# Two attention blocks in one kernel: later branch hints, early transfers awaited before the branch, and an instruction order from new costs

## The chip, the core and the metric

The kernel runs on one core of a Trainium2 chip. A core has five engines that work side by side, each on its own stream of instructions: TensorE (PE, matrix products, whose weight loads the profile lists as PEld), VectorE (DVE), ScalarE (ACT), GpSimd (POOL) and SyncE (SP, which here only issues transfers). They meet through semaphores. On-chip data lies in SBUF; products land in PSUM, which has eight banks of 128 x 512 32-bit numbers.

The metric is the device time of one execution in microseconds, lower is better. It is given as the median of several runs. Beside it stands one execution that the hardware profiler recorded; its span goes from the first to the last recorded instruction.

## The reference

Two attention blocks are computed from separate inputs, and their outputs stand side by side. Both have 2048 rows, width 1024 and 32 heads of 32.

```python
def _A_ref(x, wqkv, wo):
    qkv = transpose((x @ wqkv).reshape(B, S, 3, H, Dh), 2, 0, 3, 1, 4)
    q, k, v = qkv[0], qkv[1], qkv[2]
    p = softmax(einsum('bhqd,bhkd->bhqk', q, k) * Dh ** -0.5)
    o = einsum('bhqk,bhkd->bhqd', p, v)
    return merge_heads(o) @ wo

def _B_ref(x, wq, wk, wv, wo, beta):      # N = 4 segments of L = 512 rows
    phi = lambda t: where(t > 0, t + 1.0, exp(t))
    g = sigmoid(beta);  M = 0;  z = 0
    for s in range(N):
        p = softmax(einsum('bhqd,bhkd->bhqk', qs, ks) * scale + causal_mask)
        a_dot = einsum('bhqk,bhkd->bhqd', p, vs)
        a_mem = (phi(qs) @ M) / (phi(qs) @ z + 1e-06)
        outs.append(g * a_mem + (1.0 - g) * a_dot)
        M = M + phi(ks).T @ vs;  z = z + phi(ks).sum(rows)
    return merge_heads(outs) @ wo

return concatenate([a, b], axis=-1)
```

A is full attention over 2048 keys. B is causal attention within segments of 512 rows, plus a memory that each segment reads and then updates.

## The kernel before, in words

**Tiling.** Heads go in groups of four (g = 0 to 7), so that a group fills 128 partitions. For A a unit is a group and 256 query rows: 64 units, each with 8 pieces of 256 keys. For B a unit (a "block") is a segment and a group: 32 blocks, each in 3 pieces. A piece of scores is computed transposed, keys on the partitions, into pairs of PSUM banks: three pairs serve the scores (`PAIRS`, banks 0 to 5), and two single banks (6 and 7, the pool `side`) serve everything else, that is projections, P·V, the memory products and the output rows. ScalarE reads a pair of banks, 128 x 1024, and writes the exponentials as bf16 into a slot of `PT` (line 1097). No maximum is subtracted; instead, the reciprocals of the row sums are checked at the end against a range (`ranges`, lines 1378 on), and the result is a flag in SBUF. Where the flag is not zero every engine branches to a second, slow program that subtracts maxima (`shifted`). With the inputs here it is not entered.

**Masks and powers.** Of a B block's three pieces two are masked by VectorE (line 1107) and one by GpSimd (line 1109), after the exponential. For phi the exponential is made on VectorE, without ScalarE: `power` (lines 1127 to 1135) takes the number apart into exponent and fraction with two integer operations and evaluates a polynomial with three `scalar_tensor_tensor` steps. `b_mem` (line 857) calls it for phi(k) and phi(q), 48 times in all. `exps_dve`, the other caller, is used only for pieces listed in `off`, and that list is empty because the parameter `off` is 0; `oks` is read only to fill it.

**The order.** The kernel has no dynamic scheduling on the chip. While it is built, a planner (`Sched`) simulates the five engines with a cost for each operation, and writes each engine's stream in the order in which its simulated queue takes operations. An operation goes when its inputs are ready by the plan; among several ready ones the lowest `prio` goes first. Costs are the `cost=` of each `do(...)`, in microseconds; `dve(n)` is n x 0.00088 + 0.14 for VectorE. Semaphore waits are put in afterwards where an operation needs another engine's result, so a wrong cost does not make a wrong result, but an instruction that stands too early in its engine's stream holds up everything behind it.

Score products have priority 0. Other products by TensorE have a due position: `pos` counts finished score pieces, and a job that is due at `due` has priority 10 + (due - pos) until it has begun, and at most 4 from then on. P·V has priority 5 while fewer than 7 slots of `PT` are free, and else the parameter `pv`. The parameters that set due positions or release:

- `span`: over how many positions ahead of a group's first A scores the nine projections of its K, Q and V are spread
- `mem`, `memM`: the due position of a block's memory products (`mem` behind the block's first scores) and of its memory update (`memM` behind that)
- `od`, `ob`: the due position of the first of a segment's eight B output rows, and the step from one to the next (`out_B`)
- `wob`: the position at which the 2 MB transfer of `WoB`, the output weights of B, is issued

The list of score pieces itself (`batches`) depends on `rate`, `lead` and `b0`.

**The end of each stream.** `emit` writes for each engine: the whole stream (`play`), a wait for the flag, a load of the flag into a register (line 435), and a branch on it (line 437). In `play` a branch hint, an instruction that tells the engine's sequencer about the branch to come, is put ahead of the operation that stands `HINT[name]` places before the stream's end; where the stream is shorter than that, ahead of the first. Behind the branch SP waits until the last transfer on each of 24 channels has landed (`drain`, line 147). A transfer takes the next channel in turn and a semaphore of its own, so 24 semaphores are awaited.

## Time and profile before

| | |
|---|---|
| median of 10 runs | 1106.36 us (1105.52 to 1109.06) |
| the profiled execution's own time | 1107.8 us |
| its span | 1106.1 us |
| mean granted TensorE clock | 0.994 |
| ScalarE before its first exponential | 10.92 us |
| last exponential's end | 1098.64 us |
| operations that GpSimd, SP play | 227, 285 |
| branch hints, at us | GpSimd 0.75, SP 0.79, PE 0.87, VectorE 600.5, ScalarE 823.0 |

An execution is longer than its span because something lies around the recorded instructions. A line of instruction groups has the source line, the engine, the operation, output and inputs with their shapes, the count, the busy time and the mean duration of one, and then the engine's idle time just ahead of these instructions with what ended it. Durations of neighbours overlap, since an engine starts an operation before the one ahead has written its last results; the time from start to start is the better price of one. "ps" stands for PSUM, whatever the bank.

### The profile page before, as it was taken

How to read it: one execution, taken by the hardware profiler on the slowest of the kernel's cores; microseconds unless marked ns; L12 is line 12 of the kernel's file. 1: busy time of each engine (PE TensorE's matmuls, PEld its weight loads, DVE VectorE, ACT ScalarE, POOL GpSimd, SP SyncE). 2: the span in 40 equal slices, each digit the busy share in tenths (PEclk: the TensorE clock that was granted, in tenths of full speed). 3: DMA queues.
4: the chain of work that ended last, by engine and by line, in shares of the span. 5: the costliest groups of instructions: out<-in, count | busy, mean ns of one | idle time of the engine just before them, and what ended most of it. 6: DMA issues, size and time to landing. Idle time of an engine off the chain costs nothing.

```text
span 1106.1 us, 54139 instructions
## 1 busy us (share of the span) xinstructions
PE 1039.2 (94%) x25177; PEld 535.3 (48%) x25177; DVE 749.1 (68%) x1569; ACT 1078.7 (98%) x1188; POOL 123.0 (11%) x231
## 2 busy tenths in 40 slices
PE   8999999999999998989999998999999999899998
PEld 4545455444444444444444544445444444454544
DVE  2366657555778779877788789787856767643333
ACT  6999999999999999999999999999999999999997
POOL 2010001001002011111112111111111111100000
PEclk9999899999999999999999999999999999999999
DMA  9632533242212322243212232412142221201111
GB/s 187 103 70 46 122 69 66 46 95 58 65 31 51 58 58 49 47 81 63 60 46 50 47 74 55 87 28 56 41 70 55 37 55 27 84 32 36 36 38 64
DMA packets 213767, 67.49 MB, mean 61 GB/s; under 512 B 202786, under 2 KB 210978, under 8 KB 213538
## 3 DMA queue, kind: packets, MB, share of 16 engines
q1 hardware_dynamic: 212066, 63.07, 27.2%
q8 instruction: 198, 3.24, 1.2%
q10 hardware_dynamic: 1472, 0.92, 0.3%
q14 instruction: 31, 0.25, 0.1%
HBM read 36.70 MB, written 8.39 MB: 41 GB/s over the span
## 4 chain that ended last, share of the span: by engine, by line
ACT 66%; PE 23%; DVE 7%; DMA 2%; issue 1%; POOL 0%; SPq 0%; DVEq 0%
ACT PT L1097 65%; PE ps L717 8%; PE ps L1212 6%; PE ps L1066 5%; PE ps L1301 3%; DMA VB<-VT 1%; PE ps L1348 1%; DVE we L1133 1%; DVE we L1134 1%; DVE VT L722 1%; DMA WA<-in_A_wqkv_dram 1%; ACT OTA L1097 1%; DVE ze L1132 0%; DVE PH L1135 0%; DMA VA<-VT 0%
## 5 line engine op out<-in xcount | busy, mean ns | idle before, releaser
L1097 ACT ACTIVATE PT<-ps 128x1024 bf16<-128x1024 f32 x1164 | 1057.7, 1153 | 10.7 <-PE ps L1066 10.1
L1212 PE MATMUL ps<-PT,ones 128*32 128x256 bf16 (+2 forms) x4784 | 283.6, 268 | 0.0
L1212 PE MATMUL ps<-PT,VA 128*32 128x256 bf16 x4016 | 241.8, 274 | 3.1 <-DVE OD L1254 0.7
L1066 PE MATMUL ps<-QA,KA 32*128 32x256 bf16 x4096 | 210.4, 274 | 34.0 <-ACT PT L1097 28.7
L717 PE MATMUL ps<-xA,WA 128*32 128x512 bf16 (+1 forms) x3232 | 204.3, 371 | 5.6 <-DMA WA<-in_A_wqkv_dram 1.1
L717 PE MATMUL ps<-xB,WB 128*32 128x512 bf16 x3072 | 205.5, 383 | 4.4 <-DVE amem L913 1.0
L1066 PEld LDWEIGHTS ps<-QA,KA 32*128 32x128 bf16 x4096 | 62.7, 92 | 207.8 <-ACT PT L1097 191.6
L1212 PEld LDWEIGHTS ps<-PT,ones 128*32 128x32 bf16 x4784 | 127.8, 97 | 29.7 <-issue 13.3
L1212 PEld LDWEIGHTS ps<-PT,VA 128*32 128x32 bf16 x4016 | 106.9, 96 | 43.7 <-issue 24.0
L717 PEld LDWEIGHTS ps<-xA,WA 128*32 128x32 bf16 x3232 | 74.4, 96 | 78.3 <-issue 25.6
L717 PEld LDWEIGHTS ps<-xB,WB 128*32 128x32 bf16 x3072 | 70.9, 96 | 77.9 <-issue 33.6
L1254 DVE COPY OD<-ps 128x512 f32<-128x512 f32 x127 | 86.5, 682 | 25.7 <-PE ps L1212 25.2
L722 DVE CAST VT<-ps 128x512 bf16<-128x512 f32 x64 | 44.0, 688 | 69.5 <-PE ps L717 52.8
L1306 DVE CAST outsb<-ps 128x512 bf16<-128x512 f32 x56 | 38.6, 690 | 72.0 <-PE ps L1301 69.8
L1109 POOL TENSOR_TENSOR PT<-PT,mask 128x256 bf16<-128x256 bf16 x64 | 45.6, 713 | 354.0 <-ACT PT L1097 352.6
L722 DVE CAST KQB<-ps 128x512 bf16<-128x512 f32 x64 | 44.1, 688 | 44.3 <-PE ps L717 42.2
L1301 PE MATMUL ps<-WoB,OTB 128*32 128x512 bf16 x1024 | 66.3, 381 | 0.7 <-DVE OD L1254 0.6
L853 POOL COPY VZ<-VB 64x256 bf16<-64x256 bf16 x64 | 28.5, 446 | 344.8 <-DMA VB<-VT 322.5
L1260 DVE STREAM_TRANSPOSE OD<-Rall 128x256 f32<-128x256 f32 x127 | 55.7, 439 | 3.0
L1257 DVE STREAM_TRANSPOSE Dt<-OD 128x256 f32<-128x256 f32 x127 | 55.3, 436 | 2.0
L1212 PE MATMUL ps<-PT,VB 128*32 128x192 bf16 (+2 forms) x768 | 45.1, 243 | 9.4 <-DVE OD L1254 3.0
L1301 PE MATMUL ps<-xA,OTA 128*32 128x512 bf16 x832 | 53.2, 381 | 0.2 <-DVE outsb L1306 0.2
(111 smaller groups left out, 880.8 us busy)
## 6 DMA issues: line engine op xcount, KB each, us to landing
WB<-in_B_wk_dram SPq DMA_DIRECT2D x32, 256.0 KB, 3.0
WB<-in_B_wq_dram SPq DMA_DIRECT2D x32, 256.0 KB, 3.0
WB<-in_B_wv_dram SPq DMA_DIRECT2D x32, 256.0 KB, 3.6
out_dram<-outsb SPq DMA_DIRECT2D x63, 128.0 KB, 1.8
WA<-in_A_wqkv_dram SPq DMA_DIRECT2D x23, 256.0 KB, 3.0
WoB<-in_B_wo_dram SPq DMA_DIRECT2D x1, 2048.0 KB, 9.9
xA<-in_A_wo_dram SPq DMA_DIRECT2D x1, 2048.0 KB, 9.5
OTA<-in_A_x_dram ACTq DMA_DIRECT2D x2, 256.0 KB, 4.5
```

What stands on the lines that cost most here:

```text
L717: ins = e.matmul(self.ps[32 * c:32 * c + 32, bank, lo:hi], W[:, i, 32 * c:32 * c + 32], x(i)[:, lo:hi], start=st, stop=sp)
L722: return e.tensor_copy(dst, self.ps[:, bank, 0:n])
L853: yield do("POOL", lambda e, j=j: e.tensor_copy(self.VZ[H * j:H * j + H, j:4:2, :], V[0:H, j:4:2, 0:P]), r=[("VB", n % 2)], w=["VZ"], cost ...
L1066: ins = e.matmul(out, l, r, start=a, stop=z)
L1097: yield do("ACT", lambda e: e.activation(to, self.ps[:, pr[0]:pr[1] + 1, 0:n], ACTF.Exp, scale=sc), r=[("ps", bk) for bk in pr], w=keys, c ...
L1109: yield do("POOL", lambda e: e.tensor_tensor(d, d, m, ALU.mult), r=keys + ["mask"], w=keys, cost=0.25 + sz * 0.0014, prio=0)
L1212: ins = e.matmul(out, l, r, start=st, stop=sp)
L1254: yield do("DVE", lambda e: e.tensor_copy(OD[:, :], self.ps[:, OB, :]), r=[("ps", OB)], w=[("OD", x), ("Rb", x)], cost=dve(2 * QU), prio=0 ...
L1257: yield do("DVE", lambda e: e.transpose(Dt[:, :], Rb), r=[("Rb", x)], w=[("Dt", x)], cost=dve(QU), prio=self.par["fp"], hold=0.15)
L1260: yield do("DVE", lambda e: e.transpose(Rb.rearrange("p (a b) -> p a b", b=32), self.spread(Rc)), r=[("Rc", ui % 64)], w=[("Rb", x)], cost ...
L1301: ins = e.matmul(self.ps[32 * c:32 * c + 32, bank, lo:hi], lhs(j)[:, 32 * c:32 * c + 32], W(j)[:, lo:hi], start=st, stop=sp)
L1306: return f(self.outsb[ob][:, :], self.ps[:, bank, :])
```

## The change

Four things are changed.

1. `HINT`: TensorE's hint goes from the first operation to the 600th from the end, GpSimd's number from 999 to 230 and SP's from 999 to 250. VectorE's and ScalarE's numbers stay.
2. `drain` can leave out the last few transfers, or take only these. SP now awaits all channels but those of the three last-planned transfers ahead of the flag, and these three behind the branch.
3. Parameters: `mem` -2 to 0, `memM` 6 to 2, `span` 50 to 60, `pv` 18 to 14, `ob` 1 to 4, `od` 8 to 4, `wob` 60 to 80, `oks` (1, 4, 6) to (1, 3, 5).
4. Planned costs: a mask on VectorE, `dve(sz)` to 0.12 + sz x 0.00055 (for 256 columns 0.365 to 0.261, for 512 columns 0.591 to 0.402); a mask on GpSimd, 0.25 to 0.4 plus sz x 0.0014 (0.608 to 0.758); each of the three polynomial steps of a power, 0.57 to 0.61.

The order of all five streams is planned anew from 3 and 4.

```diff
-    def drain(self, eng):
-        last = [op for op in self.ch_last if op is not None]
-        for op in sorted(last, key=self.all.index):
+    def drain(self, eng, but=0):
+        last = sorted([op for op in self.ch_last if op is not None], key=self.all.index)
+        for op in last[but:] if but < 0 else last[:len(last) - but]:
             eng.wait_ge(self.ch_sem[op.dma], 16 * self.ch_n[op.dma])
...
-HINT = {"PE": 99999, "ACT": 300, "DVE": 700, "POOL": 999, "SP": 999}
+HINT = {"PE": 600, "ACT": 300, "DVE": 700, "POOL": 230, "SP": 250}
...
-    par = dict(b=(16, 12, 9), mem=-2, memM=6, span=50, rate=0.6, ahead=28, sl=7, pv=18, ob=1, lead=6, b0=1, bpos=16, wob=60, mg=0.05, off=0, oks=(1, 4, 6), sh=4, pd=4, o0=4, od=8,
+    par = dict(b=(16, 12, 9), mem=0, memM=2, span=60, rate=0.6, ahead=28, sl=7, pv=14, ob=4, lead=6, b0=1, bpos=16, wob=80, mg=0.05, off=0, oks=(1, 3, 5), sh=4, pd=4, o0=4, od=4,
...
                 loc = self.R.play(eng, name, HINT[name])
+                if name == "SP":
+                    self.R.drain(eng, 3)
                 self.R.after(eng, self.flagop)
                 v = eng.value_load(self.flag[0:1, 0:1])
...
                 if name == "SP":
-                    self.R.drain(eng)
+                    self.R.drain(eng, -3)
...
             if self.par["mk"][k]:
-                yield do("DVE", ... ALU.mult), ... cost=dve(sz), prio=self.par["mp"])
+                yield do("DVE", ... ALU.mult), ... cost=0.12 + sz * 0.00055, prio=self.par["mp"])
             else:
-                yield do("POOL", ... ALU.mult), ... cost=0.25 + sz * 0.0014, prio=0)
+                yield do("POOL", ... ALU.mult), ... cost=0.4 + sz * 0.0014, prio=0)
...
-        yield do("DVE", lambda e: e.scalar_tensor_tensor(w, uf, C2, uf, ALU.add, ALU.mult), ... cost=0.57, prio=pd)
-        yield do("DVE", lambda e: e.scalar_tensor_tensor(w, w, C1, uf, ALU.add, ALU.mult), ... cost=0.57, prio=pd)
-        yield do("DVE", lambda e: e.scalar_tensor_tensor(ap, w, C0, pf, ALU.add, ALU.mult), ... cost=0.57, prio=pd)
+        yield do("DVE", lambda e: e.scalar_tensor_tensor(w, uf, C2, uf, ALU.add, ALU.mult), ... cost=0.61, prio=pd)
+        yield do("DVE", lambda e: e.scalar_tensor_tensor(w, w, C1, uf, ALU.add, ALU.mult), ... cost=0.61, prio=pd)
+        yield do("DVE", lambda e: e.scalar_tensor_tensor(ap, w, C0, pf, ALU.add, ALU.mult), ... cost=0.61, prio=pd)
```

## The prediction

> **What bounds the kernel now.** I read the busy table first, then the two groups that carry most of ScalarE's and the masks' work, then the waits of ScalarE, then the run cut into stretches, and last the records of the final 8 us.

> ```profile
> PE 1039.2 (94%) x25177; PEld 535.3 (48%) x25177; DVE 749.1 (68%) x1569; ACT 1078.7 (98%) x1188; POOL 123.0 (11%) x231
> ...
> L1097 ACT ACTIVATE PT<-ps 128x1024 bf16<-128x1024 f32 x1164 | 1057.7, 1153 | 10.7 <-PE ps L1066 10.1
> ```

> ScalarE (ACT) is busy 98% of the span with the exponentials of line 1097, so nothing that the other engines do can save more than ScalarE's idle time. Its exponentials start 0.904 us after one another (median in the trace; 1153 ns is the latency of one, and they overlap). Their number and their order come from the list of score pieces, which the change leaves alone, so the busy 1078.7 us stay. What can move is where ScalarE waits:

> ```profile
> ACT PT L1097 <- PE ps L1066: 10.1, 19, 1.5
> ACT WoB L1097 <- PE ps L1066: 7.9, 2, 7.3
> ACT outsb L1306 <- PE ps L1301: 3.3, 1, 3.3
> ```

> Scores come late 19 times, 10.1 us in all, the worst time 1.5 us. The other two rows are the start (the first exponential begins at 10.92) and the tail. Cut into stretches, ScalarE's busy time beside the length shows where the idle lies:

> ```profile
> 155.00:355.00 200.00, 198.93 (x221) 1.00 0.27 59
> ...
> 515.00:660.00 145.00, 142.23 (x158) 1.00 0.24 54
> 660.00:830.00 170.00, 169.90 (x189) 1.00 0.29 58
> 830.00:876.00 46.00, 43.04 (x48) 0.96 0.27 48
> ```

> Columns are the stretch, its length, busy time (instructions), TensorE's clock, DMA share and GB/s. Idle is 1.07, 2.77, 0.10 and 2.96 us here. The span of 1106.06 is 10.92 of start, 1076.33 of exponentials, 11.39 of idle between them (9.92 of it from 125 to 1042, which is 1.08% of these 917 us) and 7.42 of tail after the last exponential at 1098.64. The profiled execution took 1107.8, 1.7 more than its span and 1.4 more than the median of the runs, 1106.36; I work out differences on the profiled execution and take them from the median.

> **What the idle is made of.** For each gap of ScalarE I looked for the last wait of TensorE (PE) before it. (a) Six times, at 387, 444, 566, 599, 652 and 875, the chain of waits goes through the steps of a power on VectorE (DVE, lines 1130 to 1135) and then a bank that VectorE hands back late; with the small gap that follows at 654 these are 3.47 us. (b) At 846 and 849, 2.66 us, TensorE waited 1.9 us for GpSimd's (POOL's) VZ, whose transfer had taken 5.17 us instead of its median 2.5. (c) At 214, 267, 329, 508, 571, 1022, 1030 and 1043, 2.5 us, TensorE never waited; other work simply stood before the scores. The rest lies at 125 to 155 and at 37.7.

> **The costs that the order is built with.**

> ```profile
> L1133 DVE SCALAR_TENSOR_TENSOR we<-ue 128x512 f32<-128x512 f32 x48 | 34.7, 722 | 0.0
> ...
> L1107 DVE TENSOR_TENSOR PT<-PT,mask 128x256 bf16<-128x256 bf16 x64 | 20.3, 316 | 7.8 <-ACT PT L1097 7.1
> L1107 DVE TENSOR_TENSOR PT<-PT,mask 128x512 bf16<-128x512 bf16 x32 | 15.0, 468 | 11.0 <-ACT PT L1097 10.8
> ```

> A power's three steps were planned at 0.57 us and now at 0.61; from start to start the trace has 0.72. So 0.04 of the missing 0.15, about a quarter, is made good. Masks on VectorE were planned at 0.365 and 0.591 and now at 0.261 and 0.402; start to start they take 0.209 and 0.342, so the surplus shrinks from 0.16 and 0.25 to 0.05 and 0.06. Masks on GpSimd go from 0.608 to 0.758; the page has a mean of 0.713 (64 of them, 45.6 us). These edits add no instruction; they move what the planner puts next to them. For group (a) the gain lies between 0 (a quarter of the error is not enough to move the bank's handback) and 3.47 (all six go). I take half, 1.7, since the cost moves the right way in each, but by less than the error.

> VectorE runs a step of a power longer when GpSimd works beside it, which no cost of either version knows:

> ```profile
> 438.67 0.43 DVE L1132 TENSOR_SCALAR ze<-ze 128x512 int32<-128x512 int32 x1
> 439.01 1.16 DVE L1133 SCALAR_TENSOR_TENSOR we<-ue 128x512 f32<-128x512 f32 x1
> 440.09 0.41 DVE L1107 TENSOR_TENSOR PT<-PT,mask 128x512 bf16<-128x512 bf16 x1
> 440.43 1.16 DVE L1134 SCALAR_TENSOR_TENSOR we<-we,ue 128x512 f32<-128x512 f32 x1
> ```

> GpSimd's masks ran from 438.83 for 0.79 and from 440.23 for 0.81. Over the run, line 1133 takes 684 ns alone (median of 39) and 873 beside a GpSimd operation (median of 9, worst 1178). [...]

> **The places.** pv 14 instead of 18 puts P·V ahead of projections that are due more than 4 positions away (before: more than 8). span 60 asks for A's projections up to 10 positions sooner. mem and memM move the memory matmuls two later and the update two sooner. od and ob spread B's output rows over 4 to 32 positions instead of 8 to 15. wob moves the 2 MB load of WoB by 20 positions, some 36 us at two exponentials each; at 117.2 it took 9.9 us to land, and it has to be there for line 1301 first at 282, so the move itself costs nothing, but the transfers behind it on SP's queue (PKt 5.9 instead of 2.5) are late at another place. oks is read only with off above zero, and off is 0: nothing. No instruction or byte is added. What all this does to the idle no row shows; the stretches bound it. At the rate of 660 to 830 (0.06%) the 917 us would have 0.5 idle, 9.4 less; at that of 515 to 660 (1.91%) 17.5, 7.6 more. Ordinary long stretches (155 to 355 has 0.54%) would give 5.0. Between these I credit half of (b), 1.3, since a transfer of twice its median is an accident of one order that another need not repeat, and 0.5 of (c), since spread output rows stand less densely before the scores at 1022 to 1043. Stretch 125 to 155 I leave as it is, with its load moved.

> **Hints.** Each is one instruction of about 50 ns. VectorE's and ScalarE's stay. GpSimd plays 227 operations, fewer than 230, so its hint stays first. SP plays 285, so its hint goes behind 35 transfers: its first transfer, issued at 0.90, comes 0.05 earlier. TensorE's leaves the front, where it was covered by the wait for VectorE's memset until 1.19, and goes among the last 600 operations, where the queue of matmuls covers it; uncovered it costs 0.05. After the branch each engine went on after 0.4 to 0.5 us already, and the last to do so is SP. Taken: -0.05, bounds -0.1 and +0.05; were a target not there, a fetch of instructions (the packets of queue 8 took 0.9 to 1.3 us near the end) would be added, +1.3.

> **The waits for transfers.** Only SP's own line matters here. Its last issue ended at 1103.52, the flag had been written at 1103.27, the load of the flag ran from 1103.58 for 0.72, the branch from 1104.34 for 0.08, and 24 waits in 12 records, 0.06 apart, and one more ran from 1104.88 to 1105.65, with the last landing at 1105.29. Now 21 waits, 0.65, stand behind the last issue and before the load, and 3 behind the branch. The load begins at 1104.2, the branch ends at 1105.06, the three waits start at 1105.52 and end near 1105.65: the same instructions in another order, with no idle time of SP to hide in. Queued behind the early waits is only the flag's load, and for that the end waits; the fourth-last landing, 1104.01, is in time. Taken: 0. Bounds: -0.35, if the flag came 0.65 later than SP's last issue (the last landing then sets the end); +0.3, if an awaited transfer landed at 1104.5, as the third-last did.

> **The sum.** -1.7 -1.3 -0.5 -0.05 +0 = -3.55; 1106.36 - 3.55 = 1102.8.

> **Rivals.** *The cushion goes (slower).* The plan now has 64 x 0.104 + 32 x 0.189 = 12.7 us less for masks and 48 x 3 x 0.04 = 5.8 more for powers: 6.9 less on VectorE, 0.22 for each of 32 B blocks, while its other operations stay underpriced (copies 0.645 for 0.59, transposes 0.47 for 0.365, reciprocals 0.237 for 0.15). The surplus on masks was what let VectorE catch up inside a B block. It decides where VectorE hands a bank back so late that TensorE's wait outlasts the two further pairs of banks of scores, 1.8 us, as at 566. If all of it passes, +6.9; if half, +3.5: 1109.8. For it: six gaps of (a) are of this kind. Against: VectorE is idle for 32% of the span. *One accident for another (no change).* Idle stays near 11 and moves; only the -0.05 remains, 1106.3. For it: all gaps are under 1.6 us at scattered places, and the ends of the kernel win nothing. Against: long stretches differ by a factor of 30. *All like 660 to 830.* -9.4, 1096.9; for it only that one stretch and 876 to 966.

> **How the numbers follow.** About 0.2%, 2.2 us, is what a measurement of this kernel tells from no change. Forecast 0.45 (1102.8, own range 1099 to 1104.1), the best stretch throughout 0.08, exchange 0.17, cushion 0.30. So faster 0.53, same 0.17, slower 0.30. The range goes from 1098, just above the best-stretch case, to 1111, past the half-passed cushion and short of the +7.6 of the worst stretch (1114.0); some 0.06 lies below and 0.12 above.

> **What would show it.** Right: ScalarE's wait for line 1066 near 6.5 us instead of 10.1, the busy time of 1097 unchanged, fewer powers in the chain before its gaps, no wait for VZ over 1 us, a tail within 0.4 of 7.42 with SP's waits partly before the flag's load. Wrong: that row at 13 or more with VectorE as the last releaser of TensorE, or a longer tail with SP waiting for a landing before the branch.

## The result, and the profile after

The changed kernel takes 1099.53 us in the median of 8 runs (1097.68 to 1100.75); the kernel before took 1106.2 in 28 runs. The ratio is 0.9936, with a 95% interval of 0.9927 to 0.9945, so 6.1 to 8.1 us are gained. The forecast was 1102.8, faster, with an own range of 1099 to 1104.1; direction and kind were right, the size was about half.

The busy table, the group of exponentials and the waits of ScalarE, after:

```profile
PE 1041.0 (95%) x25233; PEld 537.2 (49%) x25233; DVE 747.6 (68%) x1569; ACT 1077.2 (98%) x1188; POOL 127.9 (12%) x231
...
L1099 ACT ACTIVATE PT<-ps 128x1024 bf16<-128x1024 f32 x1164 | 1056.2, 1166 | 7.2 <-PE ps L1068 6.7
```

```profile
ACT WoB L1099 <- PE ps L1068: 7.3, 2, 6.6
ACT PT L1099 <- PE ps L1068: 6.7, 10, 1.3
ACT outsb L1308 <- PE ps L1303: 3.4, 1, 3.4
```

Lines have moved by two (1097 is 1099 now). ScalarE does the same work and is still what bounds the kernel. It waits for late scores 10 times instead of 19 and 6.7 us instead of 10.1; the waits of the start (row `WoB`) take 0.6 less, that of the tail (row `outsb`) 0.1 more. The stretches, with ScalarE's busy time:

```profile
155.00:355.00 200.00, 196.33 (x218) 0.98 0.29 61
...
515.00:660.00 145.00, 144.91 (x162) 1.00 0.25 57
660.00:830.00 170.00, 168.36 (x188) 1.00 0.24 55
830.00:876.00 46.00, 46.00 (x53) 1.00 0.24 55
```

The two bad stretches of before are clean: 0.09 idle instead of 2.77 from 515 to 660, and none instead of 2.96 from 830 to 876. The stretch 155 to 355 is worse, 3.67 instead of 1.07, and its clock column says 0.98; that turns out to be another cause. The stretch 660 to 830, the best of before, is worse too, 1.64 instead of 0.10, at a whole clock.

Idle time is not all that ScalarE loses. One exponential's latency is 1.17 us while the next can start 0.904 after it, so a start that is late by under a quarter of a microsecond leaves no idle time in the table. The better account is the time from the first start to the last over 0.904 us for each of the 1183 steps between the 1184 exponentials. I call it lost time. The 32 half-size pieces, whose usual spacing is 0.493, count in it as whole ones, so as an absolute loss each figure is 13.15 us too low (30.1 for before and 25.3 for after); between kernels, which all have the same pieces, the differences stand.

| | before | after | difference |
|---|---|---|---|
| first exponential starts | 10.92 | 10.38 | -0.54 |
| lost time between exponentials | 16.96 | 12.13 | -4.83 |
| last exponential's start to the span's end | 8.74 | 8.40 | -0.34 |
| span | 1106.06 | 1100.35 | -5.71 |
| the profiled execution's own time | 1107.8 | 1102.15 | -5.65 |

So the order gave most of it, in one pair of executions. The experiments take it apart.

### The profile page after: what moved, and what is told of

The parts are those of the page before. It is cut to its first block, busy times and chain, and to the rows that moved or that the text cites. A ratio compares the mean times of both kernels' runs of the same rounds, so it can differ in the third digit from the quotient of the medians.

```text
span 1100.3 us, 54247 instructions
## 1 busy us (share of the span) xinstructions
PE 1041.0 (95%) x25233; PEld 537.2 (49%) x25233; DVE 747.6 (68%) x1569; ACT 1077.2 (98%) x1188; POOL 127.9 (12%) x231
## 4 chain that ended last, share of the span: by engine, by line
ACT 82%; PE 13%; DVE 3%; DMA 1%; issue 0%; DVEq 0%
ACT PT L1099 81%; PE ps L719 5%; PE ps L1214 3%; PE ps L1068 2%; PE ps L1303 2%; DMA VA<-VT 1%; ACT OTA L1099 1%; DMA VB<-VT 0%; PE ps L598 0%; DVE VT L724 0%; DVE PH L1137 0%; ACT OTB L1099 0%; DVE we L1136 0%; DVE xA L654 0%; DMA PKt<-PH 0%
## 5 line engine op out<-in xcount | busy, mean ns | idle before, releaser
L855 POOL COPY VZ<-VB 64x256 bf16<-64x256 bf16 x64 | 30.9, 482 | 300.6 <-DMA VB<-VT 263.9
## 6 DMA issues: line engine op xcount, KB each, us to landing
WoB<-in_B_wo_dram SPq DMA_DIRECT2D x1, 2048.0 KB, 10.4
```

The lines of the kernel that those rows point to most:

```text
L855: yield do("POOL", lambda e, j=j: e.tensor_copy(self.VZ[H * j:H * j + H, j:4:2, :], V[0:H, j:4:2, 0:P]), r=[("VB", n % 2)], w=["VZ"], cost ...
```

## The experiments

**First round: the ends, the order, and the order's two halves.** Each kernel is the one before with some of the edits.

```diff
# e1_ends: the order of before
-HINT = {"PE": 99999, "ACT": 300, "DVE": 700, "POOL": 999, "SP": 999}
+HINT = {"PE": 600, "ACT": 300, "DVE": 700, "POOL": 230, "SP": 250}
+                if name == "SP":
+                    self.R.drain(eng, 3)
...
-                    self.R.drain(eng)
+                    self.R.drain(eng, -3)
# e2_order: costs and parameters of after, HINT and drain of before
# e3_costs: costs of after alone
-cost=dve(sz)            -cost=0.25 + sz * 0.0014   -cost=0.57 (three steps)
+cost=0.12 + sz*0.00055  +cost=0.4 + sz * 0.0014    +cost=0.61
# e4_places: parameters of after alone
-mem=-2, memM=6, span=50, pv=18, ob=1, wob=60, od=8
+mem=0, memM=2, span=60, pv=14, ob=4, wob=80, od=4
```

> The order of before, with only the hints and SP's early waits changed. Prediction's theory (the ends are worth about 0.05 us): 1106 us, within 1 us of before; the first exponential at 10.4 to 10.9, the tail after the last exponential 7.2 to 7.5, lost time between exponentials as before (17.0 us over 0.904 and 0.493 us from start to start). Rival (the ends give what the prediction missed, since the profile after has the first exponential 0.54 earlier and the tail 0.2 to 0.4 shorter): 1105.2 to 1105.5.

> The order of after, with the hints and the waits of before. Prediction's theory (all gain is the order): 1099.5 to 1100, lost time between exponentials 12 to 13 us as after (12.1). Rival (late hints free TensorE's and SP's fetches during the run): 1102 or more, with lost time near 15.

> New planned costs of masks and powers alone; places, hints and waits of before. Prediction's theory: powers in the chain before ScalarE's gaps become rarer, gain about 1.7 us (0 to 3.5): 1103 to 1106. Rival cushion: slower, 1108 to 1110, VectorE the last releaser before the gaps. Rival re-draw (any new order lands somewhere between 1098 and 1108): no tie to the powers.

> The new parameters alone (mem, memM, span, pv, ob, od, wob), old costs, hints and waits. Prediction's theory: gain about 1.8 us: 1104 to 1105. If costs and places add up, the gains of this run and of the one with costs alone sum to that of the order, 6 to 7 us. Rival re-draw: they do not add up, and either may be slower than before.

| | median | ratio to before, 95% interval | lost time in the profile |
|---|---|---|---|
| e1_ends | 1105.88 | 0.9986 (0.9976 to 0.9996) | 15.40 |
| e2_order | 1100.33 | 0.9949 (0.9932 to 0.9965) | 9.21 |
| e3_costs | 1105.30 | 0.9987 (0.9976 to 0.9998) | 12.57 |
| e4_places | 1112.28 | 1.0049 (1.0034 to 1.0063) | 21.50 |

The order alone brings 5.6 us (3.9 to 7.5). Its halves do not add: the costs alone bring 1.4, near the 1.7 that I gave them, but the places alone cost 5.4, where I had credited them with 1.8. One gap is larger than all of this loss. Line by line, ScalarE in the kernel with the places alone, and TensorE's chain before the score that ends the gap:

```profile
815.07 4.97 ACT L1097 ACTIVATE PT<-ps 128x1024 bf16<-128x1024 f32 x5
827.71 1.94 ACT L1097 ACTIVATE PT<-ps 128x1024 bf16<-128x1024 f32 x2 [7.67 <-PE ps L1066]
```

```profile
819.62 1.87 PE ps L1301 x32
821.48 0.02 issue
821.50 0.70 DVE outsb L1306
822.21 0.04 issue
822.25 0.62 PE ps L626 x16
822.87 1.73 PE ps L717 x32
824.60 0.11 PE ps L626 x4
824.71 2.59 PE ps L717 x48
827.29 0.36 PE ps L1066 x12
```

Here B's third segment ends. Its output rows (line 1301) stand in TensorE's stream ahead of the K and Q projections of the next block (line 717), which need the bank that the copy of an output row hands back at 822.2. The next block's scores (line 1066) need both projections, and since score pieces go in a fixed list, every later piece waits too. TensorE is busy for 12.34 of the 12.70 us from 815.0 to 827.7 (0.73 us of the chain above is line 626, products of zeros that the planner puts in where nothing is ready); it does the wrong work first.

This gap is no surprise to the planner. Its simulated ScalarE has a hole of 9.15 us at this place, and its simulated end is 1101.7, against 1094.6 for before, 1094.9 for the new costs and 1090.5 for after. (These are the planner's numbers, not the chip's.) The gap of 1.39 us at 566 in before, which I had put down to underpriced powers, is in the plan of before as well, as 1.52 at 561. That made a new theory: what the chip loses follows the idle time that the plan itself accepts, and the parameters are a lucky set for one set of costs.

**Second round: the ends apart, and two tests of the plan theory.**

```diff
# e5_hints: HINT of after alone          # e6_waits: drain(3) and drain(-3) alone
# e7_places_vmask: places of after, and of the costs only VectorE's masks
+cost=0.12 + sz * 0.00055
# e8_true: places of after, costs at the spacing in the trace
+cost=0.08 + sz * 0.0005   (masks on VectorE)
+cost=0.72                 (each step of a power)
+cost=0.4 + sz * 0.0014    (masks on GpSimd)
```

> The order of before, with only the hints of TensorE and SP moved from the front. Theory from the run with both ends changed: the start is what the hints give; first exponential at 10.4 to 10.7 instead of 10.9 to 11.05, SP's flag load still 0.72 to 0.73, end 8.7 after the last exponential's start; 1106.3 to 1106.7, 0.3 to 0.6 below before. Prediction's theory: 0.05.

> The order of before, with only SP's waits split. Theory: SP's flag load starts later, when the other engines' loads of the flag are over, and takes 0.47 instead of 0.72; the end comes 8.45 to 8.5 after the last exponential's start instead of 8.74, the first exponential stays at 10.9 to 11.05; about 0.25 below before. Prediction's theory: 0, the same instructions in another order.

> The new places, with VectorE's new mask costs as the only new cost (powers 0.57, GpSimd's masks 0.608 planned, hints and waits of before). Prediction's theory: the powers' price brings 1.7 of the gain, so 1102 or more, with gaps behind powers. Plan theory (what the chip does follows where the plan itself leaves ScalarE idle; its own end is 1094.6 for before, 1090.5 for after, 1101.7 for places alone, and 1093.1 here): no gap of 7 us near 820, 1103 to 1104.

> The new places, with the costs of masks on VectorE and of powers set to the spacing that the trace shows (0.208 and 0.336 for masks, 0.72 for a power's step), GpSimd's masks 0.758, hints and waits of before. Prediction's theory (a price nearer to the trace gives a better order): 1100 or less. Plan theory: the plan ends at 1099.2 and has a hole of 8.9 us at 817 ahead of a B block's scores, so 1108 to 1110, with a gap of 6 us or more there.

| | median | ratio to before, 95% interval | planner's end |
|---|---|---|---|
| e5_hints | 1106.44 | 0.9999 (0.9987 to 1.0011) | 1094.6 |
| e6_waits | 1106.28 | 1.0001 (0.9988 to 1.0013) | 1094.6 |
| e7_places_vmask | 1106.43 | 0.9997 (0.9987 to 1.0006) | 1093.1 |
| e8_true | 1106.29 | 1.0005 (0.9993 to 1.0018) | 1099.2 |

*Hints.* No effect that can be measured. The first exponential came at 10.94 with late hints; over all kernels it came between 10.36 and 11.05, at 10.50 with the old hints and at 10.98 with the new. The 0.54 us of the first pair of profiles was the scatter of the start.

*Waits.* In the profile the end comes 8.48 us after the last exponential's start instead of 8.74. SP's load of the flag is shorter; in the run with the split waits, and then in the one with hints alone:

```profile
L437 SPq TENSOR_LOAD <-flag x1: 472/472/472, 1103.1 to 1103.1; - x1
```

```profile
L435 SPq TENSOR_LOAD <-flag x1: 711/711/711, 1101.9 to 1101.9; - x1
```

All seven kernels with split waits have 0.47 or 0.48 here; of the seven with the old waits six have 0.71 to 0.73, and one, e8_true of the second round, 0.49. The split puts SP's load after the loads of the other four engines, but e8_true shows that this is not the only way to a short one, so why stays open. A quarter of a microsecond is too little for the timed runs: their interval is 1.0001 +- 0.0012. The 1.5 us of e1_ends (ratio 0.9986) and the 0.8 between after and the order alone, whose intervals overlap, may hold more than this quarter; neither half showed it by itself.

*Costs.* With VectorE's mask price alone added to the places the hole near 820 is gone and the time falls by 5.9 us (1112.28 to 1106.43; 5.3 by the two ratios to before), the whole loss of e4_places and no more. From there to the whole order, 1100.33, the powers' price and GpSimd's mask price bring another 6.1 (5.3 by the ratios). Part of this is TensorE's clock, of which more below: in the profile of e7_places_vmask it halves from 159.7 to 163.1, and gaps of 2.51 and 0.81 us fall on this stretch. In the runs with a mean clock of 1.000, three of e7_places_vmask (1104.74, 1104.74, 1104.79) and two of e2_order (1099.99, 1100.0), 4.7 are left. The planner's end is the same to 0.1 with and without GpSimd's price, and planned without it the order differs from that of e2_order in 51 of TensorE's 5608 operations and 2 of GpSimd's 227, and in none of the other engines. So I put this down to the powers; no run has them alone. It is more than the whole 1.7 that I had given it, and more than the 2.6 by which the planner's end falls. My expectation for e7_places_vmask, 1102 or more, was open upwards and tells little; that of the plan theory, 1103 to 1104, was too low.

*Truer costs.* They do not help by themselves. The hole that the plan has at 817 (8.89 us) is there:

```profile
825.37 1.94 ACT L1097 ACTIVATE PT<-ps 128x1024 bf16<-128x1024 f32 x2 [7.45 <-PE ps L1066]
```

The median, 1106.29, was still 2 us under what the plan theory gave: outside the hole the chip lost less than with other costs. Time minus planner's end is 7.1 here, and 9.8 to 13.3 in before, e2, e3, e4 and e7.

**What makes runs of one kernel differ.** After and e2_order have the same order, and their profiles lose 12.13 and 9.21 us. Gaps of one order recur at the same places to a few tenths from run to run, except where TensorE's granted clock halves. In the profile of after, TensorE's busy time in stretches of 3.41 us, with the granted clock:

```profile
165.99:169.40 3.41, 1.93 (x76) 1.00 0.19 38
169.40:172.81 3.41, 3.41 (x36) 0.50 0.02 5
244.49:247.90 3.41, 2.03 (x56) 1.00 0.66 121
247.90:251.31 3.41, 3.41 (x40) 0.51 1.19 220
```

The gaps of 1.34 us at 172.0, 0.91 at 249.6 and 0.58 at 252.0 lie in and right behind these two stretches and are absent, or under 0.1, where the clock stays whole. These 2.83 us of idle time are nearly all of the 2.92 that this profile lost over e2_order's.

**Third round: places searched for other costs, one place put back, and after again.** With the planner alone I searched sets of places for the costs of after and for those of e8_true, kept for each the set with the earliest planned end, and ran both.

```diff
# e9_search_true: costs of e8_true, ends of after
+mem=-2, memM=0, span=62, sl=8, pv=12, wob=50, od=6, td=46
# e10_search_new: after, with
+mem=-1, memM=1, span=56, pv=15, wob=60, od=3, td=38
# e11_od8: after, with
-od=4
+od=8
# e12_after: after
```

> Costs of masks and powers at the spacing that the trace shows (as in the run with these costs and the new places), but places searched anew for these costs, so that the plan has no hole near 820 and ends at 1092.2 instead of 1099.2; both ends as in after. If the chip adds what it added there at full clock (1106.0 against 1099.2, 6.8): 1099 at full clock, about 1100 in the median, and few gaps that the plan does not have. Prediction's theory alone (truer prices help by themselves): below 1098.

> The costs and both ends of after, places searched further (mem -1, memM 1, span 56, pv 15, wob 60, od 3, td 38): the plan ends at 1088.4 instead of 1090.5. Plan theory: 2 us below after, 1097.5 in the median. Rival (plans this near each other are told apart by nothing but luck on the chip): anywhere between 1097 and 1105.

> After with one place put back, od 8 instead of 4. Prediction's theory (places are small terms that add): within 1 us of after, 1099 to 1100.5. Plan theory: the plan ends at 1106.6 with a hole of 8.0 at 825 and one of 2.9 at 662; 1113 to 1117, with a gap of 6 us or more near 830 after which a B block's scores come.

> After itself once more, beside the three others: 1098 at full clock, 1099.5 in the median. Its gaps of 0.2 us and more stand at the same places as in the first profile, except those inside stretches of half clock, which move.

| | median | ratio to before, 95% interval | planner's end |
|---|---|---|---|
| e9_search_true | 1101.39 | 0.9951 (0.9938 to 0.9964) | 1092.2 |
| e10_search_new | 1104.43 | 0.9978 (0.9967 to 0.9988) | 1088.4 |
| e11_od8 | 1117.50 | 1.0098 (1.0080 to 1.0116) | 1106.6 |
| e12_after | 1099.19 | 0.9937 (0.9925 to 0.9950) | 1090.5 |

One place put back costs 18 us against after beside it, a little more than the plan theory's 1113 to 1117. The plan's holes of 2.91 and 8.02 us are on the chip as 2.86 at 667 and

```profile
834.09 2.85 ACT L1099 ACTIVATE PT<-ps 128x1024 bf16<-128x1024 f32 x3 [7.02 <-PE ps L1068]
```

again behind the output rows at a segment's end. So the plan tells of holes. It does not tell plans 2 us apart: the earliest planned end, e10, came out 5 us slower than after. In its profile the clock is halved three times for 3.41 us before the end, and ScalarE's worst gaps, 2.03 and 1.50 us at 356 to 362, lie there; no run of its 12 had a mean clock above 0.997. The search with truer prices brought 4.9 us over e8_true (the ends of after, which it has and e8_true has not, included), of 7.0 in the plan, but it does not beat after either; nor did any other run.

The last profile of after was taken with a whole clock, and is the cleanest of all:

```profile
ACT PT L1099 <- PE ps L1068: 2.9, 6, 0.9
```

Lost time is 8.04, the span 1096.2. Against the first profile of the same program, 4.1 us longer, 2.83 is the gaps in and behind the two stretches of half clock; the rest I have not traced.

## Why the prediction was right, and where its size came from

The forecast had the direction and the bound. That its sum also had the right sign is in part luck: of its two order terms, costs and places, the second has the wrong sign when it is tried alone.

*The bound.* Right. ScalarE has the same 1184 pieces in every kernel here (at most two neighbours change places), and what changed is when they could start. Nor is the gain only a matter of TensorE's clock: the runs with a mean clock of 1.000 have a median of 1104.74 for before (nine) and 1098.56 for after (eight), 6.2 us apart.

*(a), the powers, credited with half of 3.47.* The gaps went and the size was too small: none of the six is left in either profile of after. By e7_places_vmask and e2_order the rest of the costs is worth 5 to 6 us once the new places and VectorE's mask price are there; all costs together are worth 1.4 in the old places. Two things in my reasoning were wrong behind this. The gap at 566 was in the plan already, at the planned prices, so it was not made by what a power takes beyond its price. And the price error matters less through its size (0.04 of 0.15 us) than through what the planner then puts elsewhere. The steps that run longer beside GpSimd, 873 ns against 684 in my medians of line 1133, did not eat the credit: the gaps went all the same. Nor did every step beside GpSimd run longer. In before four of the 144 steps began within 0.2 us behind a mask of GpSimd and took 1.16 to 1.18 us; the five beside which masks began only later took 0.68 to 0.69. In after the three longest, 1.04 to 1.05, also began behind a mask, by 0.55 to 0.67 us. So the longest steps are few, four of 144 and three.

*(b) and (c), credited with 1.3 and 0.5 of 5.2.* Their gaps went too, and no wait of TensorE for VZ is left; what each was worth no run shows apart. New gaps came, so the groups cannot simply be added: in the clean profile 1.13 us lie at the end of a segment at 810 to 813. Of (b) I had misread one half. TensorE's clock was halved from 847.5 to 850.9, which is the 0.96 in my row of 830 to 876. In before, the stretch and the projections ahead of the second gap, which took 1.51 of the 2.66 us:

```profile
847.50:850.91 3.41, 3.41 (x60) 0.50 0.02 5
...
847.75 2.56 PE ps L717 x24
```

In e1_ends, the same order, VZ's transfer was as late (5.14 us) but the clock was whole there, the same 24 products took half as long, and the second gap is missing:

```profile
847.42 1.29 PE ps L719 x24
```

So the late transfer belongs to the order, as I had it, but the half clock to the execution. The eight gaps of (c) are all in the plan of before, as holes of 0.26 to 1.01 us, like the one at 566.

*The places.* This is the step that failed in kind. I had each parameter's effect as a small term to be added, and credited 1.8 us to them. Alone they cost 5.4, and taking back one of them, od, costs 18. They gained only as a set, for the costs they were chosen with. The range from the best to the worst stretch (9.4 less to 7.6 more) held e4_places, but not e11_od8, which is 11 us slower than before.

*Hints, -0.05.* Right: nothing.

*Waits, 0.* Mis-sized by about 0.25, inside its bounds: I carried the duration of SP's load over, 0.72, and behind the split waits it takes 0.47. The rest of the working, the same instructions in another order and all landings in time, held.

*Rival cushion.* It fell: costs alone were not slower. *Rival exchange* fell too for after, though e7 is an instance of it: other gaps, the same time. *What would show it:* I had asked for a wait of ScalarE near 6.5; it was 6.7 in the first profile, but of this 2.8 was half clock, and 2.9 in the last.

## What to carry to other kernels

Where an order is written out by a planner, read the planner's own idle time on the bounding engine before anything else: the large gaps that the plans contained were on the chip nearly at their size (7.67 for 9.15, 7.45 for 8.89, 7.02 for 8.02, 2.86 for 2.91, 1.39 for 1.52). Such a gap goes when the order is planned anew, as with the new mask price in e7_places_vmask; that a price is nearer to the trace does not by itself remove it, as e8_true shows. The reverse does not hold: the chip also has gaps that no plan has, as those at 356 to 362 in e10_search_new. Judge parameters of such a planner as a set with the costs, by running the set; a single parameter taken over or put back can cost more than the whole set gains. And price a bounding engine's loss by the spacing of its starts, not by its idle column, since overlapping latencies (here 1.17 us each, 0.904 apart) hide late starts.
